# Recurrence scores in blocks of eight tokens, and id scatters without mutual order, in a gated recurrence followed by a top-2 expert router

## The chip, the cores and the metric

The kernel runs on one core of a Trainium2 chip, in one launch. A core has a matmul engine (TensorE, PE in the profile, with its weight loads as PEld), three engines for elementwise work (VectorE = DVE, ScalarE = ACT, GpSimd = POOL), SyncE (SP), which here only issues transfers, and 16 DMA engines. The metric is the device time of one execution in microseconds.

## What is computed

A linear recurrence with a forget gate for 4 batches, 8 heads, 768 tokens and head dimension 48; its output, put together over heads to 3072 rows of 384, goes through a router that picks two of eight experts for each row and adds their weighted outputs. All in float32.

```python
f = 1 / (1 + exp(-f_logit))                       # (B, H, S, D)
for t in range(S):                                # recurrence, per batch and head
    state = f[t][:, None] * state + outer(k[t], v[t])
    y[t] = q[t] @ state
x = y.transpose(0, 2, 1, 3).reshape(B * S, H * D) # 3072 x 384
noisy = x @ w_gate + log1p(exp(x @ w_noise)) * noise
top2 = the two largest of noisy in each row; w = softmax over the two
out[n] = sum over the two e of  w * (relu(x[n] @ w1[e]) @ w2[e])   # 384 -> 1024 -> 384
```

## The kernel before

**Stages.** The 768 tokens of a sequence are cut into six pieces of 128 (C = 128, NCH = 6). One stage handles one piece of all four batches. weave(c, ...) runs two streams side by side, batches 0 and 2 in one, 1 and 3 in the other, so a stage is two pairs of batches. One turn of weave lets each stream take one step of chunk(c, b) and then hands some steps of expert blocks (filler) to the engines, spread evenly over the turns of the stage. After the stage, route(c) computes the logits, the top 2, the place of every row in its expert's list and writes the row numbers to those places in DRAM; choose(c) decides on VectorE which expert blocks come next. The program is emitted in exactly this order, and every engine works through its own part of it in order.

**chunk(c, b), the recurrence for one batch and one piece.** q, k and the gate logits are transposed (L208), so that head dimension lies on partitions and 4 pairs of heads x 128 tokens on 512 columns; ScalarE applies the sigmoid (L212) and copies q and k (L215, L219). The scores inside a piece are made by doubling: the diagonal by a matmul of every q with every k, multiplied by an identity (L231, L233), then seven levels of block size 1, 2, 4, ... 64 (L238). A level multiplies the q of the second half of every block pair with the k of the first half (16 recorded matmuls, L247), keeps only the pairs that belong to the level by a masked copy into the score tile A on VectorE (L255; the last level is a plain copy on ScalarE, L257), multiplies q of the second halves (qv, L253, VectorE) and k of the first halves (kv, L259, GpSimd) with the products T of the gates, and forms the next T (L261, GpSimd). The next level's matmul needs both products. After the levels, y = A v + q state (L268, L272), the new state (L281 to L303), and the rows for the router. A score tile in PSUM occupies two banks, and there are two such tiles.

**Scatters.** route(c) ends with eight indirect DMAs on GpSimd (L369), one for each batch and rank, which write token numbers to computed places of the DRAM tensor ids. They all write the same tensor, so each waits for the one before it to land.

**Expert blocks.** A block is 128 rows of one expert. fetch(c, i) loads its places from ids (L441, SyncE), its weights where they are not there already (L446, SyncE) and gathers the rows (L447, GpSimd); block(c, i) transposes the rows (L458), copies them out (xT, L460, VectorE), multiplies by w1 (L475), applies relu (L479, ScalarE), gathers the present output rows (L480, GpSimd), multiplies by w2 (L486), adds (L489, VectorE) and scatters the sum (L490, GpSimd). It has seven steps: transposes with xT, four parts of L475, two of L486. There are 55 blocks: 0, 0, 6, 8, 8, 8 of them are handed to stages 0 to 5 (in stage 2 from the seventh turn on), and 25 run after the last routing, the tail.

**Setup.** GpSimd builds six masks of 512 columns, clears buffers and issues the router's loads and the clearing of the DRAM tensors before its first part of the recurrence.

Of the kernel before, what the change touches and what calls it, by code (L numbers as in the profile page):

```python
# [8 lines left out]
F32 = mybir.dt.float32  # L9
# [11 lines left out]
def kernel(  # L21
# [30 lines left out]

    nc = tc.nc
# [4 lines left out]
    C = 128  # L58
# [3 lines left out]
    NL = 7  # L62
    HC = C // 2
    KO = DM // 128
# [9 lines left out]
    assert (H * D, 1 << NL, B * S, FO) == (DM, C, N, 8)  # L74
# [30 lines left out]

    masks = ctile([NL - 1, H * HC], "masks", U8)
    for l in range(NL - 1):
        m, nb = 1 << l, HC >> l
        mf = wk.tile([C, H * HC], F32, tag="mf", name=f"mf{l}", bufs=1)
        nc.gpsimd.memset(mf, 1.0)  # L110
        nc.gpsimd.affine_select(out=mf, in_=mf, compare_op=ALU.is_ge, fill=0.0, base=0,
                                pattern=[[0, H], [-2 * m, nb], [0, m]], channel_multiplier=1)
        nc.gpsimd.affine_select(out=mf, in_=mf, compare_op=ALU.is_ge, fill=0.0, base=m - 1,
                                pattern=[[0, H], [2 * m, nb], [0, m]], channel_multiplier=-1)
        nc.gpsimd.tensor_copy(masks[:, l], mf)
# [66 lines left out]

    state = [None] * B
    xrow = [None] * NCH
    vts = {}
# [11 lines left out]
    def chunk(c, b):  # L197
# [13 lines left out]
        fT = wk.tile([128, HP * C], F32, tag="T0", name=f"f{u}")  # L211
# [15 lines left out]
        A = wk.tile([C, 2, HP * C], F32, tag="A", name=f"A{u}")  # L227
# [5 lines left out]
        nc.vector.tensor_tensor(A.rearrange("j r (a i) -> j (r a) i", i=C), sc.rearrange("j r (a i) -> j (r a) i", i=C),  # L233
                                ident.unsqueeze(1).broadcast_to((C, H, C)), ALU.mult)
        yield

        T = fT
        for l in range(NL):  # L238
            m, nb = 1 << l, HC >> l
# [3 lines left out]
            nj = C if l < NL - 1 else HC  # L243
            sc = two_banks(f"sc{l}{u}")
            for hp in range(HP):
                for par in range(2):
                    nc.tensor.matmul(sc[0:nj, par, hp * HC:(hp + 1) * HC].rearrange("j (a m) -> j a m", m=m),  # L247
                                     lhsT=kQ[rows(par), hp * C:hp * C + nj],
                                     rhs=qv[rows(par), hp * nb:(hp + 1) * nb, :], start=True, stop=True)
            Av = A.rearrange("j r (x two m) -> j r x two m", two=2, m=m)[0:nj, :, :, 1, :]  # L250
            scv = sc[0:nj, :, 0:HP * HC].rearrange("j r (x m) -> j r x m", m=m)
            Tv = T.rearrange("d (x two) -> d x two", two=2)
            nc.vector.tensor_tensor(qv, qv, Tv[:, :, 0:1].broadcast_to((128, x, m)), ALU.mult)  # L253
            if l < NL - 1:
                nc.vector.copy_predicated(Av, masks[:, l].rearrange("j (r x m) -> j r x m", r=2, m=m), scv)  # L255
            else:
                nc.scalar.copy(Av, scv)  # L257
            if l < NL - 1 or not last:
                nc.gpsimd.tensor_tensor(kv, kv, Tv[:, :, 1:2].broadcast_to((128, x, m)), ALU.mult)  # L259
                Tn = wk.tile([128, x], F32, tag=f"T{l + 1}", name=f"T{l + 1}{u}")  # L260
                nc.gpsimd.tensor_tensor(Tn, Tv[:, :, 0], Tv[:, :, 1], ALU.mult)  # L261
                T = Tn
            yield

        y = two_banks(f"y{u}")
        for hp in range(HP):
            for par in range(2):
                nc.tensor.matmul(y[rows(par), par, cols(hp)], lhsT=vt[:, 2 * hp + par, :], rhs=A[:, par, cols(hp)],  # L268
                                 start=True, stop=(c == 0))
            if c:  # L270
                for par in range(2):
                    nc.tensor.matmul(y[rows(par), par, cols(hp)], lhsT=state[b][rows(par), hp, :],  # L272
                                     rhs=qP[rows(par), cols(hp)], start=False, stop=True)
# [34 lines left out]
    def route(c):  # L308
# [128 lines left out]
    def fetch(c, i):  # L437
# [3 lines left out]
        nc.sync.dma_start(out=pl, in_=ids[bass.ds(at, C), :])  # L441
# [85 lines left out]
    def weave(c, filler, n, first):  # L527

        turns, done, t = 2 * (NL + 3 - (c == NCH - 1)), 0, 0
# [55 lines left out]
```

## Time and profile before

| | us |
|---|---|
| median of three runs | 1368.93 |
| lowest and highest | 1366.94, 1375.6 |
| the profiled execution | 1372.28 |
| its span in the profile | 1370.6 |
| TensorE busy in it | 1086.1 |
| VectorE, ScalarE, GpSimd busy | 402.5, 187.6, 443.9 |

All durations below are those of the one profiled execution. A busy time is the sum of the records of an engine; "idle before" is what the engine stood still ahead of a group of instructions, with the work whose end released it behind the arrow. L12 is line 12 of the kernel. The granted clock (PEclk) is that of TensorE, as a share of 2.4 GHz.

### The profile page before, as it was taken

What the parts mean: (1) busy time and instruction counts of PE and PEld (TensorE: products, weight loads), DVE (VectorE), ACT (ScalarE), POOL (GpSimd) and SP (SyncE); (2) the same over time, 40 slices, a digit from 0 to 9 for tenths busy, and PEclk for the clock granted to TensorE, in tenths of its full rate; (3) what the DMA queues carried; (4) which work ended last, traced back from release to release, by engine and by line L of the source; (5) the groups of instructions that cost most, each with busy time, mean ns of one, the idle gap of its engine ahead of it and who ended that gap; (6) DMA issues with size and microseconds to landing.
All of it is one profiled execution on the core that took longest, in us unless ns stands there. A gap on an engine that the chain in (4) does not pass through costs nothing. (4 is left out here: it accounts for less than half of the span.)

```text
span 1370.6 us, 21425 instructions
## 1 busy us (share of the span) xinstructions
PE 1086.1 (79%) x8461; PEld 882.3 (64%) x8461; DVE 402.5 (29%) x1046; ACT 187.6 (14%) x322; POOL 443.9 (32%) x602
## 2 busy tenths in 40 slices
PE   3687399559997499997399997699984599999997
PEld 2686367457776477776377766477853477777775
DVE  3354244531434232423231524232413011101110
ACT  1013021202013002103001113012020000111110
POOL 9731424151341342431242431342512222222221
PEclk7566565559998689987789997699996799999999
DMA  6733030255663177542154573355630866558830
GB/s 88 285 47 70 1 48 7 48 196 150 226 213 88 58 259 183 196 142 65 42 184 74 210 235 67 114 182 173 219 122 24 305 219 217 200 200 306 316 111 1
DMA packets 188227, 201.83 MB, mean 147 GB/s; under 512 B 115024, under 2 KB 163315, under 8 KB 187104
## 3 DMA queue, kind: packets, MB, share of 16 engines
q1 hardware_dynamic: 174576, 162.15, 39.2%
q0 software_dynamic: 13552, 38.33, 8.0%
q8 instruction: 67, 1.10, 0.4%
q14 instruction: 32, 0.26, 0.1%
HBM read 213.89 MB, written 25.30 MB: 175 GB/s over the span
## 5 line engine op out<-in xcount | busy, mean ns | idle before, releaser
L475 PE MATMUL bh<-xT,w 128*128 128x128 f32 x2640 | 344.2, 293 | 58.8 <-DVE xT L460 49.7
L475 PEld LDWEIGHTS bh<-xT,w 128*128 128x128 f32 x2640 | 327.3, 206 | 73.5 <-DVE xT L460 60.3
L247 PE MATMUL sc<-qP,kQ 48*128 48x64 f32 (+1 forms) x2688 | 215.2, 329 | 125.5 <-POOL kQ L259 121.3
L486 PE MATMUL by<-w,h 128*128 128x384 f32 x880 | 300.8, 496 | 0.0
L247 PEld LDWEIGHTS sc<-qP,kQ 48*128 48x128 f32 (+1 forms) x2688 | 204.4, 241 | 140.3 <-POOL kQ L259 123.0
L486 PEld LDWEIGHTS by<-w,h 128*128 128x128 f32 x880 | 165.7, 194 | 104.9 <-issue 5.3
L490 POOL DMA_INDIRECT out_dram<-rows_out,places x55 | 56.8, 1032 | 363.8 <-DVE rows_out L489 336.3
L489 DVE SCALAR_TENSOR_TENSOR rows_out<-by,gt,rows_out 128x384 f32<-128x384 f32 x55 | 34.0, 618 | 447.2 <-PE by L486 319.8
L479 ACT ACTIVATE h<-bh 128x512 f32<-128x512 f32 x110 | 65.7, 597 | 704.7 <-PE bh L475 704.7
L259 POOL TENSOR_TENSOR kQ<-kQ,T 128x256 f32<-128x256 f32 x140 | 115.4, 824 | 124.5 <-PE sc L247 124.0
L253 DVE TENSOR_TENSOR qP<-qP,T 128x256 f32<-128x256 f32 x144 | 67.1, 467 | 279.0 <-POOL T L261 162.0
L255 DVE COPY_PREDICATED A<-masks,sc 128x512 f32<-128x512 uint8 x144 | 129.7, 900 | 0.0
L369 POOL DMA_INDIRECT ids<-tokens,ati x48 | 46.6, 970 | 230.1 <-DMA ids<-tokens,ati 131.9
L480 POOL DMA_INDIRECT rows_out<-out_dram,places x55 | 56.5, 1028 | 104.0 <-DMA out_dram<-rows_out,places 99.7
L447 POOL DMA_INDIRECT rows_in<-xd,places x55 | 56.8, 1033 | 37.0 <-issue 19.1
L231 PE MATMUL diag<-qT,kQ 48*128 48x128 f32 x384 | 34.3, 329 | 21.5 <-ACT kQ L219 21.5
L458 PE MATMUL bx<-ident,rows_in 128*128 128x128 f32 x165 | 29.3, 289 | 25.5 <-DMA rows_in<-xd,places 25.5
L231 PEld LDWEIGHTS diag<-qT,kQ 48*128 48x128 f32 x384 | 29.0, 228 | 28.5 <-ACT kQ L219 28.5
L458 PEld LDWEIGHTS bx<-ident,rows_in 128*128 128x128 f32 x165 | 21.2, 147 | 39.8 <-issue 28.5
L268 PE MATMUL y<-A,v 128*48 128x128 f32 x384 | 45.2, 337 | 0.0
L257 ACT COPY A<-sc 64x512 f32<-64x512 f32 x24 | 13.1, 578 | 228.6 <-PE sc L247 228.6
L259 POOL TENSOR_TENSOR kQ<-kQ,f 128x256 f32<-128x256 f32 x24 | 21.7, 905 | 62.7 <-PE sc L247 62.6
(135 smaller groups left out, 738.6 us busy)
## 6 DMA issues: line engine op xcount, KB each, us to landing
w<-in_moe_w_dram SPq DMA_DIRECT2D x110, 1536.0 KB
xd<-zero POOLq DMA_DIRECT2D x4, 1176.0 KB, 16.2
xd<-xrow SPq DMA_DIRECT2D x24, 196.0 KB
f<-in_f_logit_dram SPq DMA_DIRECT2D x24, 192.0 KB
q<-in_q_dram SPq DMA_DIRECT2D x24, 192.0 KB
k<-in_k_dram SPq DMA_DIRECT2D x24, 192.0 KB
v<-in_v_dram SPq DMA_DIRECT2D x24, 192.0 KB
out_dram<-zero POOLq DMA_DIRECT2D x4, 1152.0 KB, 6.3
```

Source lines behind the costliest of these rows:

```text
L231: nc.tensor.matmul(sc[:, par, cols(hp)], lhsT=kQ[rows(par), cols(hp)], rhs=qT[rows(par), cols(hp)], start=True, stop=True)
L247: nc.tensor.matmul(sc[0:nj, par, hp * HC:(hp + 1) * HC].rearrange("j (a m) -> j a m", m=m), lhsT=kQ[rows(par), hp * C:hp * C + nj], rhs=qv ...
L253: nc.vector.tensor_tensor(qv, qv, Tv[:, :, 0:1].broadcast_to((128, x, m)), ALU.mult)
L255: nc.vector.copy_predicated(Av, masks[:, l].rearrange("j (r x m) -> j r x m", r=2, m=m), scv)
L259: nc.gpsimd.tensor_tensor(kv, kv, Tv[:, :, 1:2].broadcast_to((128, x, m)), ALU.mult)
L447: nc.gpsimd.indirect_dma_start(out=xr, out_offset=None, in_=xd, in_offset=bass.IndirectOffsetOnAxis(ap=pl.bitcast(U32), axis=0), bounds_ch ...
L458: nc.tensor.transpose(xp[:, j * 128:(j + 1) * 128], xr[:, j * 128:(j + 1) * 128], ident)
L475: nc.tensor.matmul(hp[:, f * 128:(f + 1) * 128], lhsT=w1[:, j, fo * 128:(fo + 1) * 128], rhs=xT[:, j * 128:(j + 1) * 128], start=(j == 0), ...
L479: nc.scalar.activation(h[:, half * 4:half * 4 + 4, :].rearrange("p f t -> p (f t)"), hp, AF.Relu)
L480: nc.gpsimd.indirect_dma_start(out=yo, out_offset=None, in_=out, in_offset=bass.IndirectOffsetOnAxis(ap=pl, axis=0), bounds_check=N - 1, o ...
L486: nc.tensor.matmul(yp[:, 0:DM], lhsT=h[:, fo, :], rhs=w2[:, fo, :], start=(fo == 0), stop=(fo == FO - 1))
L490: nc.gpsimd.indirect_dma_start(out=out, out_offset=bass.IndirectOffsetOnAxis(ap=pl, axis=0), in_=yo, in_offset=None, bounds_check=N - 1, o ...
```

## The change

The scores inside a block of eight tokens are made by one masked matmul. For that the products of the gates inside a block are formed ahead of the middle (tile ahead) and their inverses behind it (tile back), q and k are multiplied with them, and all pairs of q and k are multiplied at once; a mask (near) keeps the pairs of the same block with the key not after the query. The block products u2 then bring q and k to the ends of the block, and only the levels 8, 16, 32 and 64 are left. The gates are kept at 2^-30 or more, so that the inverses are finite.

The products kv and T of the levels are on VectorE; GpSimd does nothing for the recurrence in the stages. The score tile A is one of four tiles kept through the kernel and cleared once, with the heads in another order; masks have 64 columns and are broadcast over heads. chunk has a step more before the first matmuls and three levels fewer, so a stage has 16 turns (14 the last) where it had 20 (18). In y the matmuls with A of all heads come before those with the state.

The eight scatters of one routing are declared independent of each other, with a memset of one column on GpSimd ahead of each, and the first load of places after them (L441) waits for all eight.

```diff
+        fT, qT, kT = wtile("fT"), wtile("qT"), wtile("kT")
         nc.scalar.activation(fT, transposed("f"), AF.Sigmoid)
-        qT = wk.tile([128, HP * C], F32, tag="qT", name=f"qT{u}")
-        qpsum = transposed("q")
-        nc.scalar.copy(qT, qpsum)
-        qP = wk.tile([128, HP * C], F32, tag="qP", name=f"qP{u}")
-        nc.vector.tensor_tensor(qP, qpsum, fT, ALU.mult)
-        kQ = wk.tile([128, HP * C], F32, tag="kQ", name=f"kQ{u}")
-        nc.scalar.copy(kQ, transposed("k"))
+        nc.scalar.copy(qT, transposed("q"))
+        nc.scalar.copy(kT, transposed("k"))
+        nc.vector.tensor_scalar_max(fT, fT, FMIN)
+        two, four = wtile("two", HP * C // 2), wtile("four", HP * C // 4)
...
+        nc.vector.tensor_tensor(two, halves(fT)[:, :, 0], halves(fT)[:, :, 1], ALU.mult)
+        nc.vector.tensor_tensor(four, halves(two)[:, :, 0], halves(two)[:, :, 1], ALU.mult)
+        qa, ka = ahead[b % 2], back[b % 2]
+        f8, q8, k8 = (x.rearrange("d (x e) -> d x e", e=MB) for x in (fT, qa, ka))
+        t4, u2 = two.rearrange("d (x e) -> d x e", e=MB // 2), halves(four)
+        nc.scalar.copy(k8[:, :, 2], f8[:, :, 3])
+        nc.scalar.copy(q8[:, :, 4], f8[:, :, 4])
+        nc.scalar.copy(k8[:, :, 1], t4[:, :, 1])
+        nc.scalar.copy(q8[:, :, 5], t4[:, :, 2])
+        nc.scalar.copy(q8[:, :, 7], u2[:, :, 1])
+        nc.vector.tensor_tensor(k8[:, :, 0], f8[:, :, 1], t4[:, :, 1], ALU.mult)
+        nc.vector.tensor_tensor(q8[:, :, 6], f8[:, :, 6], t4[:, :, 2], ALU.mult)
+        nc.vector.reciprocal(q8[:, :, 0:4], k8[:, :, 0:4])
+        nc.vector.reciprocal(k8[:, :, 4:8], q8[:, :, 4:8])
+        qM, kM, qP, kQ = wtile("qM"), wtile("kM"), wtile("qP"), wtile("kQ")
+        nc.vector.tensor_tensor(qM, qT, qa, ALU.mult)
+        nc.vector.tensor_tensor(kM, kT, ka, ALU.mult)
+        yield
...
-        sc = two_banks(f"diag{u}")
+        A = scores[(c * B + b) % 4]
+        sc = two_banks(f"near{u}")
...
-                nc.tensor.matmul(sc[:, par, cols(hp)], lhsT=kQ[rows(par), cols(hp)], rhs=qT[rows(par), cols(hp)],
+                nc.tensor.matmul(sc[:, par, cols(hp)], lhsT=kM[rows(par), cols(hp)], rhs=qM[rows(par), cols(hp)],
...
-        nc.vector.tensor_tensor(A..., sc..., ident.unsqueeze(1).broadcast_to((C, H, C)), ALU.mult)
+        for dst, x, s in ((qP, qM, 0), (kQ, kM, 1)):
+            nc.vector.tensor_tensor(eights(dst), eights(x), u2[:, :, s:s + 1].broadcast_to((128, HP * C // MB, MB)),
+                                    ALU.mult)
+        T = wtile("T8", HP * C // MB)
+        nc.vector.tensor_tensor(T, u2[:, :, 0], u2[:, :, 1], ALU.mult)
+        nc.vector.copy_predicated(A, near.unsqueeze(1).broadcast_to((C, H, C)),
+                                  sc.rearrange("j r (a i) -> j (r a) i", i=C))
         yield
 
-        T = fT
-        for l in range(NL):
+        for l, m in enumerate(LEVELS):
...
             nc.vector.tensor_tensor(qv, qv, Tv[:, :, 0:1].broadcast_to((128, x, m)), ALU.mult)
-            if l < NL - 1 or not last:
-                nc.gpsimd.tensor_tensor(kv, kv, Tv[:, :, 1:2].broadcast_to((128, x, m)), ALU.mult)
-                Tn = wk.tile([128, x], F32, tag=f"T{l + 1}", name=f"T{l + 1}{u}")
-                nc.gpsimd.tensor_tensor(Tn, Tv[:, :, 0], Tv[:, :, 1], ALU.mult)
+            if not (top and last):
+                nc.vector.tensor_tensor(kv, kv, Tv[:, :, 1:2].broadcast_to((128, x, m)), ALU.mult)
+                Tn = wtile(f"T{2 * m}", x)
+                nc.vector.tensor_tensor(Tn, Tv[:, :, 0], Tv[:, :, 1], ALU.mult)
+                T = Tn
...
+        mine = []
         for b in range(B):
             for r in range(2):
-                nc.gpsimd.indirect_dma_start(
+                nc.gpsimd.memset(pause, 0.0)
+                ins = nc.gpsimd.indirect_dma_start(
                     out=ids, out_offset=bass.IndirectOffsetOnAxis(ap=ati[:, r, b:b + 1], axis=0),
-                    in_=tokens[:, c, b:b + 1], in_offset=None)
+                    in_=tokens[:, c, b:b + 1], in_offset=None).ins
+                for other in mine:
+                    tc.declare_no_dep(ins, other, reason="distinct places")
+                mine.append(ins)
+        placed.extend(mine)
...
-        nc.sync.dma_start(out=pl, in_=ids[bass.ds(at, C), :])
+        ins = nc.sync.dma_start(out=pl, in_=ids[bass.ds(at, C), :]).ins
+        for other in placed:
+            tc.add_manual_dep(ins, other.name, ...)
+        placed.clear()
...
-        turns, done, t = 2 * (NL + 3 - (c == NCH - 1)), 0, 0
+        turns, done, t = 2 * (len(LEVELS) + 4 - (c == NCH - 1)), 0, 0
```

## Rows read from the trace of the kernel before

**Rows 1.** The page, part 1: busy us, share of the span, instructions.

```profile
PE 1086.1 (79%) x8461; PEld 882.3 (64%) x8461; DVE 402.5 (29%) x1046; ACT 187.6 (14%) x322; POOL 443.9 (32%) x602
```

**Rows 2.** Waits: engine and line, waited for; us in total, times, longest us.

```profile
POOL ids L369 <- DMA ids<-tokens,ati: 131.9, 42, 5.2
PE sc L247 <- POOL kQ L259: 121.3, 8, 29.5
```

**Rows 3.** TensorE's timeline, stage 0: start, us, group [idle before].

```profile
46.55 3.68 PE L247 MATMUL sc<-qP,kQ 48*128 48x64 f32 x32 [29.47 <-POOL kQ L259]
```

**Rows 4.** TensorE's timeline, second pair of stage 0, and the router's first matmul.

```profile
74.08 0.66 PE L208 MATMUL fp<-ident,f 128*128 128x128 f32 x4
...
88.45 14.97 PE L247 MATMUL sc<-qP,kQ 48*128 48x64 f32 x144 [0.17 <-DVE A L255]
103.67 1.12 PE L247 MATMUL sc<-qP,kQ 48*64 48x64 f32 x16 [0.25 <-POOL T L261]
104.72 3.36 PE L268 MATMUL y<-A,v 128*48 128x128 f32 x32
...
111.99 4.77 PE L316 MATMUL lg<-w_rt,yT 128*128 128x16 f32 x32
```

**Rows 5.** TensorE's timeline, second pairs of stages 3 and 4, with blocks.

```profile
590.28 2.93 PE L475 MATMUL bh<-xT,w 128*128 128x128 f32 x12 [2.17 <-DVE xT L460]
593.14 3.68 PE L247 MATMUL sc<-qP,kQ 48*128 48x64 f32 x32
596.75 7.05 PE L475 MATMUL bh<-xT,w 128*128 128x128 f32 x36
...
753.79 0.60 PE L208 MATMUL fp<-ident,f 128*128 128x128 f32 x4
...
762.46 1.60 PE L475 MATMUL bh<-xT,w 128*128 128x128 f32 x12 [1.31 <-DVE xT L460]
763.99 2.00 PE L247 MATMUL sc<-qP,kQ 48*128 48x64 f32 x32
765.93 4.29 PE L475 MATMUL bh<-xT,w 128*128 128x128 f32 x36
```

**Rows 6.** Single lines (min/median/max ns), then groups by line (busy us, mean ns).

```profile
L253 DVE TENSOR_TENSOR qP<-qP,T x144: 406/426/1014, 48.6 to 1002.0; 128x256 f32<-128x256 f32 x144
L255 DVE COPY_PREDICATED A<-masks,sc x144: 679/715/1330, 17.5 to 993.2; 128x512 f32<-128x512 uint8 x144
...
L217 DVE TENSOR_TENSOR qP<-qp,f 128x512 f32<-128x512 f32 x24 | 16.5, 688 | 20.3 <-ACT qT L215 20.3
L329 DVE MAX8 mx<-nz 128x8 f32<-128x8 f32 x24 | 3.7, 155 | 0.2
L322 ACT ACTIVATE sp<-sp 128x32 f32<-128x32 f32 x6 | 1.4, 229 | 0.1
L342 DVE RECIPROCAL sm<-sm 128x4 f32<-128x4 f32 x6 | 1.1, 178 | 0.2
L340 DVE TENSOR_TENSOR sm<-ex 128x4 f32<-128x4 f32 x6 | 1.0, 164 | 1.7 <-ACT ex L339 1.7
```

**Rows 7.** Timelines at the start of stage 3: TensorE, then VectorE behind choose().

```profile
435.81 1.09 PE L208 MATMUL fp<-ident,f 128*128 128x128 f32 x4
443.96 0.68 DVE L217 TENSOR_TENSOR qP<-qp,f 128x512 f32<-128x512 f32 x1
```

**Rows 8.** Timelines after the last routing: GpSimd, TensorE, VectorE.

```profile
1034.43 0.98 POOL L369 DMA_INDIRECT ids<-tokens,ati  x1 [12.88 <-DVE whole L390]
...
1062.02 0.97 POOL L369 DMA_INDIRECT ids<-tokens,ati  x1 [3.14 <-DMA ids<-tokens,ati]
1075.01 0.87 PE L458 MATMUL bx<-ident,rows_in 128*128 128x128 f32 x3 [20.61 <-DMA rows_in<-xd,places]
1075.71 0.62 DVE L489 SCALAR_TENSOR_TENSOR rows_out<-by,gt,rows_out 128x384 f32<-128x384 f32 x1 [34.26 <-DMA rows_out<-out_dram,places]
```

**Rows 9.** Windows: us, busy us (records) of five engines, PEclk, DMA share, GB/s.

```profile
596.00:598.00 2.00, 2.00 (x14) 1.88 (x13) 1.35 (x3) 0.00 (x0) 1.31 (x4) 0.50 0.00 0
944.00:1020.00 76.00, 70.25 (x624) 55.45 (x622) 26.35 (x53) 10.93 (x20) 26.11 (x36) 1.00 0.52 179
```

More of the change, by code (lines that the diff above doesn't have):

```diff
@@ L61 @@
     DP = 64
-    NL = 7
+    MB = 8
+    LEVELS = [8, 16, 32, 64]
     HC = C // 2
+    FMIN = 2.0 ** -30
     KO = DM // 128
@@ L104, with keep @@
             nc.vector.memset(pads[n][i][:, :, D:DP], 0.0)
[L106 to L115, printed above, removed]
+    masks = ctile([len(LEVELS) - 1, HC], "masks", U8)
+    near = ctile([C], "near", U8)
+    mf = ctile([len(LEVELS) - 1, HC], "mf")
+    nf = ctile([C], "nf")
+    nc.gpsimd.memset(mf, 1.0)
+    nc.gpsimd.memset(nf, 1.0)
+    def keep(t, base, pattern, mult):
+        nc.gpsimd.affine_select(out=t, in_=t, compare_op=ALU.is_ge, fill=0.0, base=base, pattern=pattern,
+                                channel_multiplier=mult)
+    for l, m in enumerate(LEVELS[:-1]):
+        keep(mf[:, l], 0, [[-2 * m, HC // m], [0, m]], 1)
+        keep(mf[:, l], m - 1, [[2 * m, HC // m], [0, m]], -1)
+    keep(nf, 0, [[-MB, C // MB], [0, MB]], 1)
+    keep(nf, 0, [[1, C]], -1)
+    nc.gpsimd.tensor_copy(masks, mf)
+    nc.gpsimd.tensor_copy(near, nf)
+    scores = [ctile([H, C], f"scores{i}") for i in range(4)]
+    for t in scores:
+        nc.gpsimd.memset(t, 0.0)
+    ahead = [ctile([HP * C], f"ahead{i}") for i in range(2)]
+    back = [ctile([HP * C], f"back{i}") for i in range(2)]
+    for t in back:
+        nc.vector.memset(t, 1.0)
     def iota(shape, name, pattern, mult, dtype=F32):
@@ L181, in clear @@
                                     in_=zero[:, 0:N // 128 // 4 * w])
+    pause = ctile([1], "pause")
     state = [None] * B
     xrow = [None] * NCH
+    placed = []
     vts = {}
@@ L242, in chunk @@
             kv = kQ.rearrange("d (x two m) -> d x two m", two=2, m=m)[:, :, 0, :]
[L243 to L244 removed]
+            nj = HC if top else C
+            sc = two_banks(f"sc{m}{u}").rearrange("j r (a i) -> j (r a) i", i=C)
             for hp in range(HP):
                 for par in range(2):
[L247 removed]
+                    nc.tensor.matmul(sc[0:nj, par * HP + hp, 0:HC].rearrange("j (a m) -> j a m", m=m),
                                      lhsT=kQ[rows(par), hp * C:hp * C + nj],
                                      rhs=qv[rows(par), hp * nb:(hp + 1) * nb, :], start=True, stop=True)
[L250 to L252 removed]
+            Tv = halves(T)
             nc.vector.tensor_tensor(qv, qv, Tv[:, :, 0:1].broadcast_to((128, x, m)), ALU.mult)
[L254 to L262 removed]
+            if not (top and last):
[3 more added lines that the diff above has]
+                T = Tn
+            Av = A.rearrange("j h (x two m) -> j h x two m", two=2, m=m)[0:nj, :, :, 1, :]
+            scv = sc[0:nj, :, 0:HC].rearrange("j h (x m) -> j h x m", m=m)
+            if top:
+                nc.scalar.copy(Av, scv)
+            else:
+                nc.vector.copy_predicated(Av, masks[:, l].rearrange("j (x m) -> j x m", m=m).unsqueeze(1).broadcast_to(
+                    (C, H, nb, m)), scv)
             yield
@@ L267, in chunk @@
             for par in range(2):
-                nc.tensor.matmul(y[rows(par), par, cols(hp)], lhsT=vt[:, 2 * hp + par, :], rhs=A[:, par, cols(hp)],
-                                 start=True, stop=(c == 0))
-            if c:
+                nc.tensor.matmul(y[rows(par), par, cols(hp)], lhsT=vt[:, 2 * hp + par, :], rhs=A[:, par * HP + hp, :],
+                                 start=(hp == 0), stop=(c == 0), skip_group_check=True)
+        if c:
+            for hp in range(HP):
                 for par in range(2):
                     nc.tensor.matmul(y[rows(par), par, cols(hp)], lhsT=state[b][rows(par), hp, :],
-                                     rhs=qP[rows(par), cols(hp)], start=False, stop=True)
+                                     rhs=qP[rows(par), cols(hp)], start=False, stop=True, skip_group_check=True)
         for par, copy in ((0, nc.scalar.copy), (1, nc.vector.tensor_copy)):
@@ L440, in fetch @@
         at = nc.sync.value_load(row_no[0:1, g:g + 1], min_val=0, max_val=NID - C)
-        nc.sync.dma_start(out=pl, in_=ids[bass.ds(at, C), :])
+        ins = nc.sync.dma_start(out=pl, in_=ids[bass.ds(at, C), :]).ins
+        for other in placed:
+            tc.add_manual_dep(ins, other.name, mybir.DependencyInfo(mybir.DependencyClass.Sync,
+                                                                    mybir.DependencyReason.DATA), reason="all places")
+        placed.clear()
         r = nc.sync.value_load(load_no[0:1, g:g + 1], min_val=0, max_val=E)
```

15 lines of the change are left out of this document (9 added, 6 removed).

## The prediction

> **What bounds the kernel now.** I read the busy shares first: TensorE 79% [rows 1]. That share is a mean, so next the waits: TensorE waited 121.3 us for GpSimd's product kQ (L259), in 8 waits, and GpSimd waited 131.9 us between its own id scatters (L369), 42 times [rows 2]. The TensorE timeline shows where. Each of the six stages (one 128-token piece of all four batches) has one long wait near its start; that of the first stage, 29.47 us, is the longest and has its row [rows 3]. In stages 1 to 5 GpSimd sits in the eight scatters of the routing just done, in the first it is still building masks, and the kQ products are queued behind. Outside these waits there are three kinds of stretch.
>
> *Bare pairs.* A stage runs batches 0 and 1 together, then 2 and 3. With no expert blocks woven in (stages 0 and 1, first half of stage 2: five pairs) TensorE alternates with VectorE. The second pair of stage 0 takes 74.08 to 111.99, 37.9 us [rows 4].
>
> *Pairs with blocks.* In seven pairs TensorE always has work, and an expert block stops only where its first matmul waits for the copy xT (L460) on VectorE: 1.31 us in the row shown [rows 5].
>
> *The tail.* 25 blocks, paced by TensorE. After the last routing TensorE idles 20.61 us for rows_in [rows 8]: that gather (L447) follows eight scatters on GpSimd, 1034.43 to 1062.02.
>
> **The terms.** Let R be the time of one new reciprocal over 128x256; everything else is worked out first.
>
> 1. *Stage waits.* No GpSimd instruction feeds the recurrence any more, so the waits on kQ go: -121.3 [rows 2]. The scatters still stand in front of the block gathers on GpSimd, but eight without mutual order take about 8 x 1.3 us (0.98 each [rows 8], a one-column memset and issue), and the first block update comes over 20 us after they start. If they don't overlap, see rival D.
>
> 2. *Tail.* From the last scatter's start to the block's first matmul is 1075.01 - 1062.02 = 13.0 us: landing, the new wait of the places load (L441) for all eight, that load, the gather. The last scatter moves to 1034.43 + 7 x 1.3 = 1043.5, so the block starts at 1056.5: -18.5. The added wait on SyncE has the weight loads and the q, k, f, v loads behind it; before, the load waited for the last scatter too, so all of them only come earlier.
>
> 3. *VectorE's new work.* Its multiplications cost 0.426 us for 256 columns (median) and 0.688 for 512, and 0.164 for 4 [rows 6], so about 0.16 + 1.02 ns a column; back to back, independent ones overlap by some 0.08. Per batch the preparation is: clamp 0.5 (the trace has none of 512; below 0.25 it can't be without beating two columns a ns, above it is 0.69), two 0.43, four 0.29, the two 64-column products 0.22 each, two reciprocals, qM and kM 0.69 each; with the overlaps, and 0.2 for the ScalarE copies, 2.9 + 2R, and 5.7 + 4R for a pair. The five small ScalarE copies are bounded by 0.23 (a 128x32 activation [rows 6]) and 0.6; at 0.6 they would add up to 2 us a pair. They hide behind VectorE; behind them on ScalarE stands the second batch's sigmoid, which VectorE can't take up earlier anyway. The block-of-8 step is qP and kQ (0.61 each), T 0.15 and the masked copy over 1024 columns, 1.2 from the median 0.715 of 512 (up to 2.5 from its longest, 1.33, taken while GpSimd multiplied): 2.5 in all. A level is qv, kv, T and the masked copy, 0.34 + 0.34 + 0.11 + 0.62 = 1.4, under the 1.67 that TensorE takes for one batch at the slow clock (144 records of 16 each in 14.97 us [rows 4]).
>
> 4. *Bare pairs.* New: 1.9 to the first sigmoid's end, 5.7 + 4R of preparation, 5.1 for the two block-of-8 steps (the level matmuls need their two PSUM tiles back), five level parts of 1.67 = 8.3, the last level 2.5, y 3.4, state update 4.0: 31.0 + 4R against 37.9, the last three read from [rows 4]. Five pairs: -34.5 + 20R; the one behind stage 1's choose() loses 1.6 more: -33 + 20R.
>
> 5. *Pairs with blocks.* (a) Three of seven levels go, 2.00 us each per pair [rows 5]: -6.0 in six pairs, -36. (b) weave() has 16 turns now, and in turns 1 and 9 a block begins: its xT stands on VectorE behind both preparations. The block's matmuls then start at 1.9 + 5.7 + 4R + 0.6, with the near matmuls (2.3) still to come: 10.5 + 4R against 8.67 in the row pair 753.79 to 762.46 [rows 5]: +1.8 + 4R in three second pairs. At a stage's start VectorE is first free after choose(), 8.15 us in [rows 7]; there it is +4.6 + 4R, three times. Together +19 + 24R. (c) In stages 3 and 4 the turns also put a block's start right behind levels 8 and 32 and behind y: stalls of 2.2, 2.2 and 1.5 where one of 2.2 was: 4 x 3.7 = +15; in stage 5 four steps a turn hide them, -4. (d) After a 2.2 us stall the granted clock fell from its 2.4 GHz level to 0.50, that is 1.2 GHz, and 12 records took 2.93 us, not 1.60, 32 took 3.68, not 2.00, 36 took 7.05, not 4.3 [rows 5, 9]: 5.8 us. I put 5.8 on turn 9 of three pairs and half of it on one more stall in each of the four pairs of stages 3 and 4: +29. (e) The pair of stage 2 has no block start in turn 9: -7 + 4R. Sum +16 + 28R; I use +15 + 28R.
>
> All: -121 - 18.5 - 33 + 15 + 48R = -157.5 + 48R.
>
> **R.** The only reciprocal in the trace is 128x4, 178 ns [rows 6]. Lower end: one column a cycle like a multiplication, 0.43. Upper end: if its fixed part is that of MAX8 (155 ns for 8 columns, 147 without them), 31 ns are left for 4 columns, 7.8 each: 2.14. I take its distance from the multiplication of 128x4 two instructions before (L340, 164 ns), the same tile and shape: 14 ns over 4 columns, 3.5 more each: 0.43 + 256 x 3.5 ns = 1.32. Then 48R = 63.4 and the sum is -94. The profiled execution took 1372.3 (span 1370.6); its median neighbour is 3.4 lower, so 1372.3 - 94 - 3.4 = 1275.
>
> The Trainium skill speaks against this step: "VectorE: DVE Perf Modes", section on the fixed hardware budget, says that the reciprocal is an iterative divide with a repeat count of 8. Read as eight cycles a column that is an estimate of 2.3 us, and the sum by it would be -47, 1322. The trace's 178 ns neither shows nor excludes it.
>
> **The rivals.**
> A. *The reciprocal runs at a column a cycle* (R = 0.43). For: 178 ns is only 14 more than the multiplication, and a fixed extra would explain them. Then -157.5 + 20.6 = -137: 1232.
> B. *It takes the upper end* (R = 2.14): VectorE's preparation of a pair is 14.3 us and nothing of TensorE's fits under it. -157.5 + 102.7 = -55: 1314. This is also the skill's rule as a mechanism of this kernel.
> C. *Slower: the clock.* The longer stalls keep TensorE at 1.2 GHz in the pairs with blocks. TensorE's work in an undisturbed pair at 2.4 GHz is 70 us now [rows 9], some 65 without three levels, 455 in seven. My sum holds 29 us of new slow time. From 1275 to 1383 it takes 108 more, that is 24% more of the 455 at half clock; above that it decides. For: 2.2 us of waiting was enough once [rows 5, 9]. Against: the stalls come three or four times in a pair of 85 us, with 8 us of loss each at most.
> D. *The scatters keep their order,* by their queue or by a dependence that stays. Then the first block's update (L489) waits on VectorE for a gather behind them, as it did 34.26 us in the tail [rows 8], with the recurrence behind it: the tail's 18.5 are not won and some 12 us come back in each of stages 3 to 5: 1275 + 55 = 1330.
>
> **How the numbers follow.** Forecast (R from 0.9 to 1.7) 0.40; A 0.20; B 0.30; C 0.05; D 0.05. The likeliest gives 1275. The range takes in both ends of R (1232, 1314) and the clock term (d) left out at the one end or nearly doubled at the other: 1225 to 1335; C, the outer part of D, and the tails of A and B lie outside, some 0.15 to 0.2. About 1% is what a measurement of this kernel can tell from no change: 1355 to 1383. All of A and nearly all of the forecast, B and D lie below: faster 0.89; same 0.06 from the edges of B and D; slower 0.05 from C.
>
> **What would show it.** Right: no wait of TensorE over 10 us in stages 1 to 5 for GpSimd; scatters about 1.3 us apart; L458's block after the last routing starting within 4 us; VectorE busy up by 60 to 140 us; the longest TensorE waits at kM (the first matmuls of a pair) and at xT in turns 1 and 9. A reciprocal of 128x256 gives R directly, and the time should move by 48 times its distance from 1.32. Wrong: scatters still 4 us apart (D); a granted clock near 0.6 over stages 3 to 5 (C); or bare pairs longer than 40 us with R small, which would mean that ScalarE's copies or PSUM tiles, not VectorE, set the pace.

## The result, and the profile after

The changed kernel takes 1252.48 us (median of four runs, 1242.77 to 1255.98), 0.912 times the kernel before (95% interval 0.906 to 0.919): 8.8% faster. The predicted 1275 lies 23 us above, inside the time's range of 1225 to 1335. The profiled execution has a span of 1248.8 against 1370.6, 121.8 less; sums below are made on spans, comparisons of runs on ratios to the kernel before on the same chip. Percentages between two runs are differences of these ratios, and 1% is 13.7 us.

Page of the changed kernel, part 1 (to be read beside [rows 1]):

```profile
PE 972.1 (78%) x7309; PEld 802.6 (64%) x7309; DVE 490.1 (39%) x1352; ACT 213.5 (17%) x442; POOL 246.5 (20%) x314
```

Groups of VectorE's instructions in it, shapes kept apart (busy us, mean ns of one, idle before):

```profile
L261 DVE RECIPROCAL ahead<-back 128x256 f32<-128x256 f32 x24 | 42.1, 1753 | 1.2 <-ACT back L256 1.2
L262 DVE RECIPROCAL back<-ahead 128x256 f32<-128x256 f32 x24 | 40.7, 1695 | 0.0
L289 DVE COPY_PREDICATED scores<-near,near 128x1024 f32<-128x1024 uint8 x24 | 31.1, 1296 | 30.9 <-PE near L282 30.9
```

R is 1.72 on average, not 1.32. VectorE has 87.6 us more in all, and the reciprocals alone take 82.8; TensorE has 114 less.

TensorE's waits in the changed kernel (us in total, times, longest; near is the masked product inside blocks of eight, bx an expert block's transposes, bh and by its products with w1 and w2):

```profile
PE bh L544 <- issue: 86.8, 7, 15.5
PE bh L544 <- DVE xT L529: 56.5, 44, 4.0
PE near L282 <- DVE kM L265: 44.5, 10, 10.0
...
PE bx L527 <- DMA rows_in<-xd,places: 16.5, 3, 14.8
PE fp L233 <- DMA f<-in_f_logit_dram: 12.5, 2, 8.3
```

The 121.3 us for kQ [rows 2] are gone and nothing on GpSimd has taken their place. The new waits are the first matmuls of a pair (near, for kM) and the first matmul of a block (bh). The label "issue" says only that the profile shows no releaser; the timelines do. At the start of stage 3, TensorE, then VectorE (start, us, group, idle before):

```profile
352.91 1.09 PE L233 MATMUL fp<-ident,f 128*128 128x128 f32 x4
...
373.51 0.77 PE L544 MATMUL bh<-xT,w 128*128 128x128 f32 x2 [15.33 <-issue]
```

```profile
361.02 0.42 DVE L243 TENSOR_SCALAR fT<-fT 128x512 f32<-128x512 f32 x1
...
362.52 1.75 DVE L261 RECIPROCAL ahead<-back 128x256 f32<-128x256 f32 x1
364.19 1.69 DVE L262 RECIPROCAL back<-ahead 128x256 f32<-128x256 f32 x1
...
372.26 0.68 DVE L265 TENSOR_TENSOR kM<-kT,back 128x512 f32<-128x512 f32 x1
372.86 0.55 DVE L529 COPY xT<-bx 128x384 f32<-128x384 f32 x1
```

VectorE comes out of choose() at 361.0, prepares both batches without a gap until 372.9, and only then copies xT, whose transposes TensorE had finished at 358.2. That is step (b). It occurs six times (15.33, 10.75, 15.37, 10.74, 15.45, 9.88 us, 77.5 in all); the seventh of the 86.8 is the wait behind the last choose(), 9.23.

Stage by stage (from the first fp of a stage to that of the next, us):

| | 0 | 1 | 2 | 3 | 4 | 5 | rest |
|---|---|---|---|---|---|---|---|
| before | 119.9 | 126.6 | 185.2 | 206.6 | 201.9 | 186.9 | 339.5 |
| after | 89.6 | 96.7 | 162.4 | 191.2 | 198.2 | 171.3 | 335.2 |
| difference | -30.3 | -29.9 | -22.9 | -15.4 | -3.7 | -15.6 | -4.3 |
| of it the wait on kQ | -30.5 | -23.0 | -19.1 | -15.3 | -21.4 | -11.9 | |

After the last routing, GpSimd, SyncE and TensorE of the changed kernel (compare [rows 8]):

```profile
916.89 0.98 POOL L430 DMA_INDIRECT ids<-tokens,ati  x1 [12.76 <-DVE whole L455]
918.18 0.96 POOL L430 DMA_INDIRECT ids<-tokens,ati  x1 [0.19 <-issue]
...
925.81 0.97 POOL L430 DMA_INDIRECT ids<-tokens,ati  x1 [0.19 <-issue]
941.93 0.34 SPq L506 DMA_DIRECT2D places<-ids  x1
944.73 1.05 POOL L516 DMA_INDIRECT rows_in<-xd,places  x1 [17.95 <-DMA places<-ids]
950.94 0.87 PE L527 MATMUL bx<-ident,rows_in 128*128 128x128 f32 x3 [14.75 <-DMA rows_in<-xd,places]
```

The scatters are issued 1.27 us apart, as forecast. But the load of places goes out 16.1 us after the last of them, not at once: from the first scatter to the block's first matmul it is 34.1 us, against 40.6 before, where 22.1 was forecast. (The rest column, -4.3, is this gain of 6.5 less 2.3 that the blocks behind it take longer.)

### The profile page after: what moved, and what is told of

It is laid out like the page before. It is cut to its first block, busy times and chain, and to the rows that moved or that the text cites. A ratio compares the mean times of both kernels' runs of the same rounds, so it can differ in the third digit from the quotient of the medians.

```text
span 1248.8 us, 18962 instructions
## 1 busy us (share of the span) xinstructions
PE 972.1 (78%) x7309; PEld 802.6 (64%) x7309; DVE 490.1 (39%) x1352; ACT 213.5 (17%) x442; POOL 246.5 (20%) x314
## 5 line engine op out<-in xcount | busy, mean ns | idle before, releaser
L544 PE MATMUL bh<-xT,w 128*128 128x128 f32 x2640 | 351.3, 297 | 143.3 <-issue 86.8
L555 PE MATMUL by<-w,h 128*128 128x384 f32 x880 | 293.9, 487 | 0.0
L555 PEld LDWEIGHTS by<-w,h 128*128 128x128 f32 x880 | 162.8, 190 | 102.1 <-issue 0.2
L303 PE MATMUL sc<-qP,kQ 48*128 48x64 f32 (+1 forms) x1536 | 117.7, 319 | 8.7 <-DVE scores L289 4.5
L303 PEld LDWEIGHTS sc<-qP,kQ 48*128 48x128 f32 (+1 forms) x1536 | 109.5, 228 | 22.1 <-issue 8.3
L307 DVE TENSOR_TENSOR qP<-qP,T 128x256 f32<-128x256 f32 x96 | 40.5, 421 | 94.3 <-PE sc L303 94.2
L282 PE MATMUL near<-qM,kM 48*128 48x128 f32 x384 | 35.2, 345 | 44.5 <-DVE kM L265 44.5
L282 PEld LDWEIGHTS near<-qM,kM 48*128 48x128 f32 x384 | 30.9, 245 | 48.2 <-DVE kM L265 47.3
L318 DVE COPY_PREDICATED scores<-masks,sc 128x512 f32<-128x512 uint8 x72 | 50.8, 705 | 0.0
L289 DVE COPY_PREDICATED scores<-near,near 128x1024 f32<-128x1024 uint8 x24 | 31.1, 1296 | 30.9 <-PE near L282 30.9
L316 ACT COPY scores<-sc 64x512 f32<-64x512 f32 x24 | 13.2, 579 | 174.4 <-PE sc L303 174.4
L261 DVE RECIPROCAL ahead<-back 128x256 f32<-128x256 f32 x24 | 42.1, 1753 | 1.2 <-ACT back L256 1.2
L527 PE MATMUL bx<-ident,rows_in 128*128 128x128 f32 x165 | 28.9, 286 | 16.9 <-DMA rows_in<-xd,places 16.5
L262 DVE RECIPROCAL back<-ahead 128x256 f32<-128x256 f32 x24 | 40.7, 1695 | 0.0
L527 PEld LDWEIGHTS bx<-ident,rows_in 128*128 128x128 f32 x165 | 20.6, 145 | 29.9 <-issue 22.1
```

Of the source, the lines that this page charges most:

```text
L261: nc.vector.reciprocal(q8[:, :, 0:4], k8[:, :, 0:4])
L282: nc.tensor.matmul(sc[:, par, cols(hp)], lhsT=kM[rows(par), cols(hp)], rhs=qM[rows(par), cols(hp)], start=True, stop=True)
L303: nc.tensor.matmul(sc[0:nj, par * HP + hp, 0:HC].rearrange("j (a m) -> j a m", m=m), lhsT=kQ[rows(par), hp * C:hp * C + nj], rhs=qv[rows(p ...
L318: nc.vector.copy_predicated(Av, masks[:, l].rearrange("j (x m) -> j x m", m=m).unsqueeze(1).broadcast_to((C, H, nb, m)), scv)
L527: nc.tensor.transpose(xp[:, j * 128:(j + 1) * 128], xr[:, j * 128:(j + 1) * 128], ident)
L544: nc.tensor.matmul(hp[:, f * 128:(f + 1) * 128], lhsT=w1[:, j, fo * 128:(fo + 1) * 128], rhs=xT[:, j * 128:(j + 1) * 128], start=(j == 0), ...
```

## The experiments

Theory: the time is TensorE's path through waits on VectorE; the gain is the vanished wait on kQ, and what stands against it is the preparation, with its reciprocals, ahead of the first matmuls of a pair and of a block's xT. The rivals stand with each experiment.

**One part of the change alone, on the kernel before.** First the scatters without mutual order:

```diff
+                nc.gpsimd.memset(pause, 0.0)
+                ins = nc.gpsimd.indirect_dma_start(...).ins
+                for other in mine:
+                    tc.declare_no_dep(ins, other, reason="distinct places")
...
+        for other in placed:
+            tc.add_manual_dep(ins, other.name, ...)
```

> The kernel before with one part of the change: the eight scatters without mutual order; seven levels, kQ products still on GpSimd. Theory: GpSimd leaves the scatters some 10 us after their start instead of 35, so the five stage waits of TensorE for kQ behind them (90 us in the trace of before) shrink to under 3 us each and the clock lost behind them comes back; the mask wait of stage 0 (29.5 us) stays; the tail gains 6 as in the changed kernel: about 1275 (1260 to 1290). Rival: the gain hangs on taking the products off GpSimd, since DMA descriptors and products still share that engine: waits of 10 us and more stay, 1330 or above.

Measured: 1321.22 us, ratio 0.965 (0.961 to 0.969). Neither theory nor rival: the gain is half of what the theory gave. TensorE's waits of this kernel:

```profile
PE sc L249 <- POOL kQ L261: 32.9, 7, 27.4
...
PE diag L233 <- issue: 18.8, 4, 7.2
```

88.4 us of the wait on kQ are gone, although kQ is still on GpSimd; what is left is mainly stage 0, where the masks are built. But the span fell only by 59.1. Of the 29.3 between the two, 18.8 stand at diag, nearly all before the second batch's at the start of stages 2 to 4, and 8.6 at level matmuls behind the masked copies. So in stages 1 to 5 it was the eight scatters' waiting on each other, not GpSimd's arithmetic, that held the recurrence.

Then the products alone:

```diff
-                nc.gpsimd.tensor_tensor(kv, kv, Tv...
+                nc.vector.tensor_tensor(kv, kv, Tv...
...
-                nc.gpsimd.tensor_tensor(Tn, Tv[:, :, 0], Tv[:, :, 1], ALU.mult)
+                nc.vector.tensor_tensor(Tn, Tv[:, :, 0], Tv[:, :, 1], ALU.mult)
```

> The kernel before with the other part: kQ and T products of all seven levels on VectorE, scatters still in order. Theory: TensorE's 121 us of waits for kQ go, but VectorE's add of a block (L489) now meets the gather behind 35 us of scatters with the whole recurrence behind it: some 10 us come back in stages 3 to 5, and 0.45 us more of VectorE a batch and level costs 30 to 45: about 1325 (1305 to 1345). Rival: the order of scatters doesn't matter once the products are off GpSimd: 1290 or below.

Measured: 1308.8 us, ratio 0.955 (0.951 to 0.959), at the lower end of the theory's range. All of the wait on GpSimd's kQ is gone, the span fell by 64.9, and TensorE's timeline shows what took its place (two of four such rows, one in each of stages 2 to 5; the others are 8.79 and 12.19):

```profile
424.88 0.90 PE L458 MATMUL bx<-ident,rows_in 128*128 128x128 f32 x3 [14.33 <-DMA rows_in<-xd,places]
...
624.89 0.90 PE L458 MATMUL bx<-ident,rows_in 128*128 128x128 f32 x3 [16.87 <-DMA rows_in<-xd,places]
```

The recurrence no longer waits for the scatters, so the block woven into it does: its gather stands behind them on GpSimd. The waits at bx rose from 25.5 to 72.6 us. This is rival D's mechanism in a kernel where the scatters keep their order, though at another place: D and the theory of this run named VectorE's add of a block (L489), and it is TensorE that waits, for the gathered rows. The products now on VectorE cost less than the theory's 30 to 45 us: TensorE waits 13.4 us for them (kQ 11.2, T 2.2).

Both together:

> Both parts together without the blocks of eight: seven levels, products on VectorE, scatters without order. What it lacks to the changed kernel is the masked matmul with its preparation. Theory: all stage waits go, nothing of the 48 reciprocals is paid, three more levels are: 1285 (1265 to 1305), so that the blocks of eight bring 30 us or less of the 118. Rival: the blocks of eight are the main gain: 1330 or above.

Measured: 1280.41 us, ratio 0.934 (0.930 to 0.937), as expected. 3.5% and 4.5% alone, 6.7% together: they remove the same wait. The rest of the change brings the other 2.1% (29 us). That rest is not the blocks of eight alone: the changed kernel also issues the matmuls of y with A of all heads first and those with the state after, where this run, like the kernel before, alternates the two kinds four by four. The y matmuls alone in the first pair of stage 3, of this run and then of the changed kernel (us of the window, busy us and records, granted clock of the window):

```profile
393.40:488.54 95.14, 5.74 (x64) 0.83 0.60 182
...
352.91:448.42 95.51, 4.11 (x64) 0.83 0.58 182
```

Over all pairs the y matmuls take some 18 us less of TensorE's time (72.3 in both kernels with the old order, 54.4). No run has the blocks of eight without the new order of y, so how the 29 us divide between the two stays open.

**The order of the scatters put back into the changed kernel** (the declare_no_dep lines left out).

> The changed kernel with the scatters waiting for each other again, the rest unchanged. Theory: TensorE's stage waits don't come back as waits for GpSimd products, but the first block update of stages 3 to 5 meets its gather behind the scatters and VectorE stands in it: 8 to 14 us in each of three stages, and the tail gets its 6 us back: 1252 + 40, 1280 to 1300. Rival: with the recurrence off GpSimd the order costs the tail alone: 1260 or below.

Measured: 1276.71 us, ratio 0.936 (0.929 to 0.943): 2.4% worse than the changed kernel, between theory and rival. Of the 27.5 us of span, 22.2 are waits at bx:

```profile
PE bx L525 <- DMA rows_in<-xd,places: 38.7, 5, 18.8
```

Only 4.0 of the 22.2 lie in the tail (18.77 against 14.75); the rest are the first blocks of stages 2 to 5 (1.85, 5.70, 6.31, 6.07). So the edit of the scatters is worth its price, in the stages rather than in the tail.

**Half the scatters,** to see what the 16.1 us between the last scatter and the places load are.

```diff
-            for r in range(2):
+            for r in range(1):
```

> The changed kernel with the four scatters of the second rank left out, so the token numbers of second choices are missing and those rows are not computed. In the tail of the changed kernel the last of eight scatters is issued 8.9 us after the first, but the load of places goes out only 15 us later. Theory: the transfers are worked off one after another at some 3 us each, so with four the load goes out 11 to 13 us earlier, 12 us or less after the first scatter starts. Rival: a landing takes 12 to 15 us however many there are: 5 us earlier, by four issues of 1.27.

Measured: 1219.61 us (one run). GpSimd and SyncE after the last routing:

```profile
903.24 0.98 POOL L430 DMA_INDIRECT ids<-tokens,ati  x1 [13.38 <-DVE whole L455]
...
907.07 0.97 POOL L430 DMA_INDIRECT ids<-tokens,ati  x1 [0.19 <-issue]
...
914.91 0.34 SPq L506 DMA_DIRECT2D places<-ids  x1
```

The load goes out 11.7 us after the first scatter, against 25.0 with eight: 13.4 earlier, as the theory said, 3.3 for each scatter. They are issued 1.27 apart and finish some 3.3 apart, so their landing, not their issue, is the limit: the median from issue to landing is 3.8 us in the kernel before, 12.3 in the changed one and 7.2 here. Giving up the order among them saves 4.9 us of 29.9 (29.9 is the same distance in the kernel with the order put back, 940.52 to 970.41). What the 3.3 us go to is not recorded: from 928 to 941 the changed kernel's profile has no DMA packet at all. Of this kernel's 31 us of span, 13.7 lie in the stages ahead of the first scatter and 3.8 behind the block's start; it also moves fewer rows (187 MB against 202), so these say nothing on the scatters.

**The reciprocals, twice.**

```diff
-        nc.vector.reciprocal(q8[:, :, 0:4], k8[:, :, 0:4])
-        nc.vector.reciprocal(k8[:, :, 4:8], q8[:, :, 4:8])
+        for _ in range(2):
+            nc.vector.reciprocal(q8[:, :, 0:4], k8[:, :, 0:4])
+            nc.vector.reciprocal(k8[:, :, 4:8], q8[:, :, 4:8])
```

> The changed kernel with both reciprocals of every batch done twice; the result is the same. They take 1.75 and 1.69 us, 3.3 us a batch back to back, 79 us over 24 batches. Theory: the preparation is on TensorE's path in every pair, so nearly all of it shows: 1252 + 70 to 80, 1325 to 1332. Rival: in the pairs with blocks other work covers part of it: 1290 or below.

Measured: 1320.43 us, ratio 0.964 (0.960 to 0.968), 5.2% or 71 us above the changed kernel for 81 us of added reciprocals: a little under the theory's 1325 to 1332 and far from the rival's 1290. The waits that grew are the two named ones (86.8 and 44.5 in the changed kernel):

```profile
PE bh L545 <- issue: 126.1, 7, 22.2
PE near L283 <- DVE kM L266: 76.6, 11, 12.6
```

**The reciprocals replaced by products,** the other direction.

```diff
-        nc.vector.reciprocal(q8[:, :, 0:4], k8[:, :, 0:4])
-        nc.vector.reciprocal(k8[:, :, 4:8], q8[:, :, 4:8])
+        nc.vector.tensor_tensor(q8[:, :, 0:4], k8[:, :, 0:4], f8[:, :, 0:4], ALU.mult)
+        nc.vector.tensor_tensor(k8[:, :, 4:8], q8[:, :, 4:8], f8[:, :, 4:8], ALU.mult)
```

> The changed kernel with both reciprocals of a batch replaced by products of the same shape (so the decayed q and k, and with them the output, are not the reference's; all else runs as it did). A 128x256 product should take 0.43 us where the reciprocals took 1.75 and 1.69, so VectorE has 48 x 1.29 = 62 us less. Doubling the reciprocals showed 86% of what it added. If they lie on the path in that share, 1190 to 1205 us. Rival: TensorE's own work or ScalarE's copies take over once they are gone, so that less than 40 us show: 1212 us or more.

Measured: 1214.68 us, ratio 0.884 (0.878 to 0.889): 2.9% or 39 us below the changed kernel, 30.1 in span, for 62 us less on VectorE by the single lengths (58 of busy time). The rival's bound is met, barely, and the place is plain. (Its scores are not the reference's, so rows can go to other experts, and it moves 208 MB against 202; in stage 3 the traffic is the same, 161 and 162 GB/s.) Windows over stages 0 and 1, then 3, first of the changed kernel, then of this one (us; busy us and records of PE, PEld, DVE, ACT, POOL; granted clock):

```profile
4.21:190.56 186.35, 132.09 (x1193) 117.89 (x1193) 130.60 (x308) 50.04 (x112) 29.73 (x53) 0.70 0.50 102
...
352.91:544.13 191.22, 145.33 (x1165) 120.46 (x1166) 80.50 (x230) 34.17 (x73) 33.53 (x40) 0.87 0.53 162
```

```profile
4.14:169.13 164.99, 128.42 (x1193) 114.65 (x1193) 111.94 (x308) 50.08 (x112) 31.12 (x53) 0.72 0.55 115
...
330.93:523.01 192.08, 150.70 (x1165) 125.31 (x1166) 70.74 (x230) 34.16 (x73) 34.41 (x40) 0.85 0.52 161
```

In the bare pairs of stages 0 and 1 the 20.7 us taken off come back whole (186.35 to 164.99). In stages 2 to 5 some 41 are taken off and only about 9 come back; in stage 3 nothing: VectorE is 9.8 us less busy, and TensorE takes 5.4 us longer over the same 1165 records, at a lower granted clock. Over the whole kernel the wait "issue" fell by 30.2 and that of near for kM by 22.0, those at xT, at bx and for f rose by 11, and TensorE's busy time rose by 10.8.

**The block's steps ahead of the recurrence's in each turn.**

```diff
+            t += 1
+            while done < min(n, n * (t - first) // (turns - first)):
+                next(filler, None)
+                done += 1
             for x in list(streams):
                 if next(x, streams) is streams:
                     streams.remove(x)
-            t += 1
-            while done < min(n, n * (t - first) // (turns - first)):
-                next(filler, None)
-                done += 1
```

> The changed kernel with one edit in the weaving: in each turn the steps of expert blocks are emitted ahead of the recurrence steps. Theory: the waits of 10 to 15 us in turns 1 and 9 exist because the copy xT stands behind both preparations on VectorE (77 us in six places); with xT ahead of them TensorE has the block's matmuls and the next turn's to do meanwhile: 40 to 60 us of the 77 go, 1195 to 1215. Rival: TensorE waits as long, now at the first near matmuls for kM: 1245 or above.

Measured: 1229.62 us, ratio 0.903 (0.895 to 0.911): 1.0% below the changed kernel, with overlapping intervals, so the ratio alone does not show a gain; it lies between theory and rival. The profiled execution's span is 19.2 us shorter. TensorE's waits:

```profile
PE bh L544 <- DVE xT L529: 88.7, 49, 7.8
...
PE bx L527 <- DMA rows_in<-xd,places: 29.4, 4, 14.1
PE bh L544 <- issue: 9.9, 2, 9.2
PE by L555 <- ACT h L548: 6.8, 3, 3.0
```

The waits of bh fell from 143.3 to 100.3, but bx took 12.9 of that back and by (L555), for relu and other work on ScalarE, 12.2: the theory named the right stall and left out that the block, now earlier, meets its gather.

**The preparation emitted two steps before its batch's turn,** with its PSUM tiles and loads; a stage then has two turns fewer.

```diff
+            if top and b % 2 == 0:
+                prep(*follower(c, b))
             yield
...
+        if b % 2:
+            prep(*follower(c, b))
         yield
```

> The changed kernel with the preparation of a batch (transposes, sigmoid, inverses, qM, kM) emitted two steps ahead, in the last level and y steps of the batch before it in its stream, also across the routing; a stage has two turns fewer. Theory: VectorE's 12.6 us of preparation a pair run while TensorE does y, the state update, routing and blocks: most of the 77 us in turns 1 and 9 and 5 to 8 us in each of five bare pairs go, 1150 to 1180. Rival: VectorE is as full in those turns and TensorE waits at xT or y instead: 1220 or above.

Measured: 1213.01 us, ratio 0.887 (0.880 to 0.893): 2.6% below the changed kernel, the lowest ratio among the kernels that compute the whole output, and yet between theory and rival. Its waits:

```profile
PE bh L569 <- DVE xT L554: 76.0, 43, 9.0
PE bx L552 <- DMA rows_in<-xd,places: 37.6, 5, 13.8
...
PE bh L569 <- issue: 26.9, 6, 9.2
...
PE near L303 <- DVE kM L267: 11.9, 2, 6.0
```

Near lost 32.6 us and bh 40.4, of which bx took 21 back and smaller waits some 25 (those for f gave back 9.5): again the scatters are next, 4.2 to 7.5 us in each of stages 2 to 5.

**Two further steps from there.** One reciprocal over three of its four columns (the fourth divides 1 by 1):

```diff
-        nc.vector.reciprocal(q8[:, :, 0:4], k8[:, :, 0:4])
+        nc.vector.reciprocal(q8[:, :, 0:3], k8[:, :, 0:3])
```

> The kernel with the preparation emitted two steps ahead, its first reciprocal over 3 of each 8 columns instead of 4 (the fourth divides 1 by 1 and is set once at the start). VectorE has 24 x 0.43 = 10 us less. If the preparation still holds the path there in part, 1203 to 1210 us against 1213; if emitting it ahead has hidden it, no change: 1211 to 1215.

Measured: 1221.92 us, ratio 0.890 (0.883 to 0.896): no gain over the 0.887 before it. The 9.6 us that VectorE saves don't show there. The row of this reciprocal is of use below. And this together with the block's steps first:

> The same, and in each turn the block's steps are emitted ahead of the recurrence's. The two edits alone brought 39 and 23 us. If each removes stalls of its own, 1185 to 1195 us. Rival: both remove the same stalls (a block's xT behind the preparation), and the block that then starts earlier waits for its gather behind the scatters: 1205 us or more.

Measured: 1231.67 us, ratio 0.897 (0.891 to 0.903): the rival. The two edits' gains don't add; the ratio is even above that of the preparation ahead alone, with overlapping intervals. Bx is now the longest wait, and bh, 102.9 us in all with the preparation ahead, still has 97.9, of which 23.5 end with the last steps of choose() (load_no and go):

```profile
PE bx L552 <- DMA rows_in<-xd,places: 53.4, 5, 13.3
PE bh L569 <- DVE xT L554: 41.4, 39, 2.5
```

## Why the prediction was right, and which steps of it were not

Sign, mechanism and range were right; the forecast came out 28 us too slow in span (-94 against -121.8) because errors of both signs lie in its sum: 33 us too low and 61 too high. That it came so near is in part luck. By its own terms:

| term | forecast | measured |
|---|---|---|
| 1. stage waits | -121.3 | -121.3, all gone |
| R, for 48 reciprocals | 1.32 | 1.72: +19 |
| 2. tail | -18.5 | -4.3: +14 |
| 4. five bare pairs, with R = 1.72 | +1.4 | -16.3: -18 |
| 5. seven pairs with blocks, with R = 1.72 | +63 | +19.9: -43 |

*Stage waits.* Right in size, with an incomplete cause. The prediction put them down to GpSimd's products queued behind the scatters, which is what the rows say, but priced only taking the products away. Either half of the change alone removes most of them; in each case a new wait keeps part of the gain (diag and the masked copies, or bx).

*R.* The step that failed is the fixed part. Two lengths are now measured: 192 columns take 1353 ns,

```profile
L263 DVE RECIPROCAL ahead<-back 128x192 f32<-128x192 f32 x24 | 32.5, 1353 | 3.0 <-ACT back L258 3.0
```

and 256 take 1753. That is 6.25 ns a column and 153 fixed, and by it four columns take 178: exactly the row that the prediction had [rows 6]. It subtracted from the 178 a multiplication (164, thus 3.5 a column more) or MAX8 (147, thus 7.8); a fixed part six ns off moves R by 0.4 us when 4 columns are carried to 256. A slope from one short row was worth no more than its two ends, and 1.72 lies between the forecast and B. By the prediction's reading of the Trainium skill ("VectorE: DVE Perf Modes", section on the fixed hardware budget: an iterative divide with a repeat count of 8) the estimate was 2.3 us; the trace, with 1.75 and 1.69, doesn't agree with that reading. A column costs 6.1 times the 1.02 ns of a multiplication's, not eight times.

*The tail.* The order left the issue, as forecast, but "landing" was taken as one fixed wait behind the last scatter. With eight in flight the landings come about 3.3 us apart. Rival D asked whether the scatters overlap; the answer is that their issue does and their landing hardly does. The sign named for it, a block start within 4 us, did not come: that matmul waited 14.75.

*Bare pairs.* The second pair of stage 0, from which the term was read, takes 37.66 us (44.12 to 81.78), where the formula with the measured R gives 37.9. The 18 us lie in stage 1 (6.8 beside its stage wait) and in the first half of stage 2 (9.7 beside its own, where +1.6 was forecast). Two things that the sum has at nothing explain most of it. In stage 0 there is no state yet, so the row pair of 37.9 [rows 4] has no y matmuls with the state; from stage 1 on they are there, and in their new order, a part of the change that got no term, they take 2.9 us less in each pair of stage 1. The y matmuls of its second pair, before and after:

```profile
194.71:239.60 44.89, 9.62 (x64) 0.62 0.26 36
...
136.89:177.95 41.06, 6.71 (x64) 0.63 0.30 40
```

And the first half of stage 2 isn't bare. With 16 turns the blocks fall otherwise over the stage than with 20, and half of the first half's bh matmuls move to the second, before and after:

```profile
250.59:339.09 88.50, 13.24 (x96) 0.65 0.42 136
...
190.56:250.19 59.63, 5.89 (x48) 0.69 0.43 154
```

The 7.4 us are a gain of term 4, and most of them (5.1, in the second half) a cost of term 5.

*Pairs with blocks.* The stalls were forecast well: 21.3 us from a stage's start to the block's matmuls with R = 1.72 (measured 20.6) and 15.1 in turn 9 (13.9). Idle time other than the old stage waits rose by 73 in the six pairs of stages 3 to 5, against 71. What failed are (a), (d) and the order of y, TensorE's own work. Windows of the six pairs, all engines, then the level matmuls and the y matmuls alone, before:

```profile
sum 561.91, PE 476.13 PEld 381.16 DVE 183.36 ACT 73.17 POOL 181.43; mean PE 79.35 PEld 63.53 DVE 30.56 ACT 12.20 POOL 30.24
...
sum 561.91, PE 90.95 PEld 84.82; mean PE 15.16 PEld 14.14
...
sum 561.91, PE 34.67; mean PE 5.78
```

and after:

```profile
sum 528.09, PE 417.64 PEld 344.15 DVE 226.62 ACT 83.80 POOL 97.13; mean PE 69.61 PEld 57.36 DVE 37.77 ACT 13.97 POOL 16.19
...
sum 528.09, PE 43.58 PEld 40.27; mean PE 7.26 PEld 6.71
...
sum 528.09, PE 24.64; mean PE 4.11
```

TensorE has 58.5 us less in them, where (a) and (d) together gave 7. The levels lost 47.4, not 36: before, the 224 level records of a pair took from 13.2 us at a granted clock of 1.00 to 18.2 at 0.80, and the forecast had priced the removed ones near the first. The y matmuls lost 10.0, which no term has. And (d) added 29 us of new slow time, but left out that the slow time behind each old stage wait goes with it: in the first pairs of the three stages the granted clock was 0.80, 0.81 and 0.81 before and is 0.83, 0.80 and 0.87, in the second pairs it was 0.92, 0.98 and 1.00 and is 0.92, 0.87 and 0.91. New and old about cancel, and rival C found nothing to stand on.

*The slope.* "48 times its distance from 1.32" holds upwards for the most part (71 of 81 us with the reciprocals doubled), and downwards only in the bare pairs. Rival A's 1232 was the price of a saving that TensorE's clock and the gather partly eat: the run with products in their place stands at a ratio of 0.884, 39 us below the changed kernel where 48 x 1.29 is 62.

What stays open: which of the two, the clock or the closer packing, makes TensorE's records longer when stalls go; why the second reciprocal of a batch takes 58 ns less than the first over the same columns; what takes the 3.3 us for a scatter of 128 numbers; and how the 29 us that the two other parts leave divide between the blocks of eight and the order of y.

## What to carry to other kernels

When a long wait goes, ask which transfer or copy its engine was hiding: here the gather behind the scatters was next, and it grew as waits ahead of it went (waits at bx: 16.5 us in the changed kernel, 37.6 with the preparation ahead, 53.4 with the blocks first too). A new preparation on an in-order engine costs most through what stands behind it there, so emit it where nothing urgent follows; two steps earlier brought 2.6%. A stall added among work that fills TensorE costs most of its length (47 of 55 us in stages 2 to 5 with the reciprocals doubled), one removed there may bring a fifth of it. And give every part of a change a term, the plain-looking ones too: the order of the y matmuls had none, and they take some 18 us less of TensorE's time.

## What the runs showed of the hardware

- A reciprocal on VectorE takes 153 ns and 6.25 for each column (128x4 178 ns, 128x192 1353, 128x256 1753), six times a multiplication's 1.02.
- Eight scatters of 128 numbers each, issued 1.27 us apart, finish about 3.3 us apart, with no DMA packet recorded in the last 13 us of it: 25.0 us from the first issue until the dependent load goes out, 11.7 with four.
- The clamp over 128x512 (L243) took 0.42 us in the median (0.52 on average, one of 2.06) where a multiplication of that size takes 0.69; the prediction had put it at 0.5.
- The 64 y matmuls of a pair take 5.74 us where two kinds alternate four by four and 4.11 where each kind runs sixteen at a time, in stages 3 to 5 at a granted clock of 1.00 (one pair before, with a stretch below it, 5.98).
- TensorE's time for the same 1165 records of stage 3 varied from 145.3 to 150.7 us with the stalls around them, at a granted clock of 0.87 and 0.85.
